# Attention in a fused attention and experts kernel: smaller array pieces for scores and values, v in longer packets, TensorE's work of an iteration in two long runs

## The chip, the cores and the metric

The kernel runs on one core of one Trainium2 chip. The metric is the device time in microseconds of one execution. TensorE (PE) does matmuls and transposes and writes PSUM; VectorE (DVE) and ScalarE (ACT) read PSUM and do the elementwise work; GpSimd (POOL) copies and clears in SBUF; SyncE (SP) issues most DMAs.

## The reference

Attention inside chunks of 64 positions, then a top-1 mixture of experts over the tokens.

```python
# q, k, v: [8 batches, 8 heads, 576 positions, 64]; chunks of 64 positions
scores = scale * np.matmul(q_c, k_c.transpose(0, 1, 2, 4, 3))
scores = scores - np.max(scores, axis=-1, keepdims=True)
attn = np.exp(scores)
attn = attn / (np.sum(attn, axis=-1, keepdims=True) + 1e-09)
out = np.matmul(attn, v_c)                       # -> x: [8, 576, 512]
# experts: 8 of them, w1 512x1024, w2 1024x512
logits = x @ w_gate
local_gate = 1.0 / (1.0 + np.exp(-(x @ w_local)))
# per token: its own best expert, or the previous token's where local_gate >= 0.5
h = np.maximum(x[b, s] @ w1[e], 0.0)
out[b, s] = p[e] * (h @ w2[e])
```

## The kernel before

The 4608 tokens are 18 blocks of 256 (`NS`), each of four 64-position chunks. Attention runs as a software pipeline over blocks. In iteration i of the loop (lines 780 to 796, i from 1 to 15) stand: scores of block i+1 (`s`), transposes of the probabilities of block i (`tp`), values of block i-1 (`va`), transposes of q and k of block i+2 (`tq`, `tk`), transposes of the output x of block i-2 (`tx`), the router's logits of block i-3 (`ra`), and the regrouping copy of q and k of block i+3 (`pr`). A string of such names (`PAR["steady"]`) is the order in which the pieces are written down, and each of PE, DVE, ACT and POOL executes its own part in that order. SP's order is made by the scheduler. At the end of an iteration q and k of block i+4 and v of block i+1 are loaded, in some iterations a quarter of an expert's weights, and in iterations 4 to 11 one half of a w1 piece is split into a high part (ACT, line 101) and a low part (DVE, line 102). The names `h0` to `h3` are places at which the steps of the routing of the first half are put in, from iteration 11 on.

Scores (line 202): for a pair of heads the transposed q of a chunk is the stationary operand, 128 rows (two heads of 64) by 64 columns. The transposed k is laid out in `kbd` as a block diagonal: head 0 in rows 0 to 63 and columns 0 to 63, head 1 in rows 64 to 127 and columns 64 to 127, the rest zeros. One matmul of 128 columns gives both heads. Two chunks go to output partitions 0 to 63 and 64 to 127. Values (line 248) are built alike: probabilities of two chunks as the contraction's 128 rows, and `v` with zero blocks and two columns of ones for each half (`DV` = 66, 132 columns a head pair of chunks); the column of ones gives the sum by which `norm` divides. The zeros and ones are written once by POOL at the start (lines 491 to 500); the loads of v fill the rest in packets of 256 bytes.

Each quarter of transposes (four of 128 x 128) fills one of three PSUM buffers (`ps_tr`), and a copy takes it out (line 161). `o`, the output of the values, is one PSUM tile for four heads, used twice a block: the second half may start when `norm` has read the first. `sc`, the scores, is one tile.

Before the loop a longer order string (`PAR["start"]`) plays the first blocks; after it `PAR["drain"]` mixes the last blocks with the first expert's work; then come the expert tiles, 507 us, to the end.

Of the kernel before, what the change touches and what calls it, by code (L numbers as in the profile page):

```python
# [8 lines left out]
F32 = mybir.dt.float32  # L9
# [15 lines left out]
P = 128  # L25
# [4 lines left out]
DV = D + 2  # L30
TA = 18
# [23 lines left out]
    "p0": "AVAAAVVV",  # L55
    "p1": "AAVA",
    "p2": "PAAA",
    "p3": "PPVP",
    "t0": "VVAVAA",
    "t1": "AAAAVA",  # L60
    "t2": "AAVAVA",
    "steady": (
        "s*4 tp*3 va h0 tp*3 va tp*2 va*2 ra h1 tk*8 s*4 tq s tq*7 va ra va tx*2 va*2 h2 pr*3 h3 tx s "
        "tx*5 pr "
    ),
# [5 lines left out]
def tile_attention_then_moe(ctx: ExitStack, tc, q, k, v, wg, wl, w1, w2, out):  # L71
# [13 lines left out]
    wg9 = cpool.tile([P, 4, 32], F32, name="wg9")  # L85

# [51 lines left out]
    def load_v(i):  # L138
        vt = vbuf[i % NV]
        for ch in range(4):  # L140
            t0 = 256 * i + 64 * ch
            b, s0 = t0 // S, t0 % S
            nc.sync.dma_start(
                vt[64 * (ch // 2):64 * (ch // 2) + 64, ch % 2, :, ch // 2, 0:D],
                v[b, :, s0:s0 + 64, :].rearrange("h s d -> s h d"),
            )
        return vt

    def pair_heads(qk, engs, parts=1):
        hd, fns = [], []  # L150
        w = 4 // parts
        dsts = [pe2.tile([P, 4, 2, 2, D], F32, name=nm + "r", tag=nm + "r", bufs=1) for nm in "qk"]
        for g in range(0, 4, w):
            for n in range(2):
                sv = qk[n].rearrange("p (hp j) (r d) -> p hp j r d", j=2, r=2)
                for r in range(2):
                    fns.append(lambda n=n, g=g, sv=sv, r=r: evac(
                        engs[len(engs) // parts * (g // w) + 2 * n + r] if parts > 1 else engs[2 * n + r],
                        dsts[n][:, g:g + w, r], sv[:, g:g + w, :, r]))
        return dsts, fns  # L160
# [24 lines left out]
    def qk_transposes(hd, qT, kbd, engs=None):  # L185
# [3 lines left out]
        kv = kbd.rearrange("a h c j (p r) -> a h c j p r", r=2)  # L189
        for r in range(2):  # L190
            atoms += trans4(
                lambda n, r=r: hd[0][:, n, r].rearrange("p j d -> p (j d)"),
                [(engs[r], qv[:, :, :, r], lambda ps: ps)], fine)
        for r in range(2):
            atoms += trans4(
                lambda n, r=r: hd[1][:, n, r].rearrange("p j d -> p (j d)"),
                [(engs[2 + 2 * r + j], kv[64 * j:64 * j + 64, :, :, j, :, r],
                  lambda ps, j=j: ps[64 * j:64 * j + 64].rearrange("a h (c p) -> a h c p", c=4))
                 for j in range(2)], fine)
        return atoms  # L200

    def scores(qT, kbd, pr, fine=False):
        sc = ps_s.tile([P, 4, 2, 2, D], F32, name="sc")

        def group(hp, cc):
            for cp in range(2):
                ch = 2 * cc + cp
                nc.tensor.matmul(  # L208
# [21 lines left out]
        def shift():  # L230
            top(0, 16)
            down(0, 16)
# [773 lines left out]
```

## Time and profile before

| what | value |
|---|---|
| median of 3 runs | 738.26 us (737.48 to 740.91) |
| profiled execution | 740.17 us, span 738.4 us |
| start, to the loop's first scores | 28.66 us |
| attention loop, 15 iterations | 152.25 us |
| drain | 50.09 us |
| experts | 507.40 us |
| one iteration in the middle (118.34 to 128.58 us) | 10.24 us |

The table's lower rows are stretches between instructions in the timeline, in the profiled execution. In the profile PE stands for matmuls and transposes, PEld for loading stationary operands (it overlaps PE). A row of the timeline merges neighbouring instructions of one kind on one engine: start, time from the first's start to the last's end, what it writes and reads, how many. `128*64` is the size of the array piece, rows by columns, and the next numbers are the moving operand. The end of a matmul includes the way through the array, so a stretch of work is read from one row's start to the next row's start.

### The profile page before, as it was taken

How to read it: one execution, taken by the hardware profiler on the slowest of the kernel's cores; microseconds unless marked ns; L12 is line 12 of the kernel's file. 1: busy time of each engine (PE TensorE's matmuls, PEld its weight loads, DVE VectorE, ACT ScalarE, POOL GpSimd, SP SyncE). 2: the span in 40 equal slices, each digit the busy share in tenths (PEclk: the TensorE clock that was granted, in tenths of full speed). 3: DMA queues.
4: the chain of work that ended last, by engine and by line, in shares of the span. 5: the costliest groups of instructions: out<-in, count | busy, mean ns of one | idle time of the engine just before them, and what ended most of it. 6: DMA issues, size and time to landing. Idle time of an engine off the chain costs nothing. (4 is left out here: it accounts for less than half of the span.)

```text
span 738.4 us, 14770 instructions
## 1 busy us (share of the span) xinstructions
PE 697.4 (94%) x4442; PEld 537.0 (73%) x4442; DVE 386.3 (52%) x853; ACT 302.6 (41%) x486; POOL 164.0 (22%) x191
## 2 busy tenths in 40 slices
PE   4899999999999999999999999999999999999982
PEld 3677666667677788686888887778887888777861
DVE  4555667777678465455323364563487332455320
ACT  3777777766532144153222441532463222432210
POOL 6110111023004122232212132322234111232100
PEclk9999999999999999999999999999999999999986
DMA  8989999997653114544111154441176310234100
GB/s 197 202 173 239 232 230 228 238 238 168 192 176 112 48 46 133 171 143 142 60 32 52 39 154 159 144 140 60 46 243 205 108 60 31 67 123 158 34 33 15
DMA packets 102918, 97.34 MB, mean 132 GB/s; under 512 B 42672, under 2 KB 79536, under 8 KB 102768
## 3 DMA queue, kind: packets, MB, share of 16 engines
q1 hardware_dynamic: 96608, 75.70, 41.0%
q0 software_dynamic: 6160, 19.85, 7.9%
q8 instruction: 69, 1.13, 0.7%
q14 instruction: 81, 0.66, 0.3%
HBM read 76.48 MB, written 19.56 MB: 130 GB/s over the span
## 5 line engine op out<-in xcount | busy, mean ns | idle before, releaser
L663 PE MATMUL y<-w2h,hp 128*128 128x512 f32 x608 | 204.7, 407 | 10.0 <-DVE hp L613 6.1
L649 PE MATMUL h<-w1h,xp 128*128 128x512 f32 x608 | 178.3, 403 | 0.0
L663 PEld LDWEIGHTS y<-w2h,hp 128*128 128x128 f32 x608 | 115.7, 191 | 39.1 <-DVE hp L613 8.3
L649 PEld LDWEIGHTS h<-w1h,xp 128*128 128x128 f32 x608 | 111.4, 189 | 23.9 <-ACTq L887 0.2
L663 PE MATMUL y<-w2l,hp 128*128 128x512 f32 x304 | 121.8, 401 | 0.0
L722 POOL DMA_INDIRECT out<-ysb,sidx x38 | 41.2, 1085 | 275.2 <-DVEq L887 187.9
L649 PE MATMUL h<-w1l,xp 128*128 128x512 f32 x304 | 95.8, 396 | 0.0
L612 ACT CAST hp<-tr 128x512 fp32r<-128x512 f32 x76 | 41.2, 589 | 107.3 <-PE tr L610 101.1
L613 DVE TENSOR_TENSOR xp<-tr,xp 128x512 fp32r<-128x512 f32 x39 | 27.0, 692 | 104.6 <-ACTq L887 67.1
L721 DVE TENSOR_SCALAR ysb<-y,ppr 128x512 f32<-128x512 f32 x35 | 26.2, 748 | 94.1 <-PE y L663 81.0
L649 PEld LDWEIGHTS h<-w1l,xp 128*128 128x128 f32 x304 | 57.1, 188 | 14.6 <-DVEq L887 0.4
L663 PEld LDWEIGHTS y<-w2l,hp 128*128 128x128 f32 x304 | 58.2, 191 | 12.4
L702 ACT ACTIVATE hsb<-h 128x1024 f32<-128x1024 f32 x35 | 35.9, 1027 | 66.9 <-PE h L649 64.3
L635 ACT ACTIVATE pex<-pex 128x8 f32<-128x8 f32 x38 | 8.0, 210 | 120.8 <-DVE pex L634 120.8
L613 DVE TENSOR_TENSOR hp<-tr,hp 128x512 fp32r<-128x512 f32 x76 | 49.3, 686 | 13.5 <-ACT hp L612 10.1
L257 PE MATMUL o<-v,pT 128*64 128x132 f32 x576 | 54.0, 293 | 1.8 <-DVE xs L272 1.8
L102 DVE TENSOR_TENSOR w1l<-raw,w1h 128x1024 fp32r<-128x1024 f32 (+1 forms) x29 | 41.0, 1433 | 19.7 <-ACT w1h L101 19.7
L166 POOL COPY qr<-qt 128x512 f32<-128x512 f32 x31 | 18.2, 616 | 127.8 <-PE tr L174 84.9
L616 POOL DMA_INDIRECT xg<-x_d,gidx x36 | 36.7, 1020 | 41.1 <-issue 23.4
L208 PE MATMUL sc<-kbd,qT 128*64 128x128 f32 x576 | 40.9, 287 | 5.1 <-ACT kbd L164 4.4
L257 PEld LDWEIGHTS o<-v,pT 128*64 128x64 f32 x576 | 30.0, 135 | 18.5 <-issue 17.2
L164 ACT COPY kbd<-tr 64x512 f32<-64x512 f32 x53 | 31.5, 622 | 22.0 <-PE tr L174 15.9
(177 smaller groups left out, 903.4 us busy)
## 6 DMA issues: line engine op xcount, KB each, us to landing
raw<-in_moe_w SPq DMA_DIRECT2D x72, 512.0 KB, 3.8
x_d<-xs SPq DMA_DIRECT2D x18, 521.0 KB, 4.1
v<-in_v SPq DMA_DIRECT2D x72, 128.0 KB, 5.8
qt<-in_q SPq DMA_DIRECT2D x11, 512.0 KB
kt<-in_k SPq DMA_DIRECT2D x11, 512.0 KB, 7.9
qt<-in_q SPq DMA_DIRECT2D x6, 256.0 KB, 6.6
kt<-in_k SPq DMA_DIRECT2D x6, 256.0 KB, 7.4
qt<-in_q SPq DMA_DIRECT2D x4, 384.0 KB
```

The lines of the kernel that those rows point to most:

```text
L102: (lo_eng or nc.vector).tensor_tensor(lo, raw, hi.bitcast(F32), ALU.subtract)
L164: eng.copy(dst, src)
L208: nc.tensor.matmul(sc[64 * cp:64 * cp + 64, hp, :, cc, :], qT[:, hp, 64 * ch:64 * ch + 64], kbd[:, hp, ch], start=True, stop=True,)
L257: nc.tensor.matmul(o[64 * cp:64 * cp + 64, hh, 0:2 * DV], pT[:, h, 64 * cp:64 * cp + 64], vt[:, cp, h].rearrange("p c d -> p (c d)"), star ...
L612: return [tr, lambda: nc.scalar.copy(hi, box["ps"]), lambda: V.tensor_tensor(lo, box["ps"], hi.bitcast(F32), ALU.subtract)]
L613: lambda: V.tensor_tensor(lo, box["ps"], hi.bitcast(F32), ALU.subtract)]
L616: nc.gpsimd.indirect_dma_start(out=dst, out_offset=None, in_=src, in_offset=bass.IndirectOffsetOnAxis(ap=gidx[t].bitcast(U32), axis=0))
L649: nc.tensor.matmul(hs[:, j], xs[a][:, c], W1[w][c][:, 512 * j:512 * j + 512], start=(c == 0 and n == 0), stop=(c == 3 and n == 2))
L663: nc.tensor.matmul(y, hx[f // 4][a][:, f % 4], W2[w][c][:, f % 2, :], start=(f == 0 and n == 0), stop=(f == 7 and n == 2))
L702: nc.scalar.activation(hsb, hs.rearrange("p j f -> p (j f)"), AF.Relu)
L721: either(mix, lambda: V.tensor_scalar(ysb, y, pr, None, ALU.mult), lambda: y_mixed(ysb, y, ym, pr))
L722: nc.gpsimd.indirect_dma_start(out=out, out_offset=bass.IndirectOffsetOnAxis(ap=sidx[t].bitcast(U32), axis=0), in_=ysb, in_offset=None, bo ...
```

## The change

Scores. k is transposed into a plain `kT`, and each head is a matmul of its own on a piece of 64 rows and 64 columns: 32 matmuls of 64 moving columns instead of 16 of 128. The two heads of a pair write different PSUM banks (`sc` has the head index j first). The pairing of heads changes from (2n, 2n+1) to (n, n+4).

Values. A position pair is split into r = 0 and 1, so that a piece has 32 rows. v has no zero blocks; two positions lie side by side with a column of ones before and after, `1 + 64 + 64 + 1` columns, and each matmul takes 65 of them: the sum of r = 0 falls into the first column, that of r = 1 into the last. Four small matmuls with `tiny` open each half and put 1e-9 there. 64 matmuls of 65 columns and 8 small ones stand for 16 of 132. `norm` adds the two sums (a reduce of two) in place of adding the 1e-9. v is loaded as eight DMAs of 64 KB in packets of 512 bytes in place of four of 128 KB in packets of 256.

Probabilities. `pr` has two buffers instead of one; subtracting the maximum is four instructions of 256 columns, because the result is written in the order that the 32-row pieces need.

Order. In the loop the values' first half comes first, then scores, router, the values' second half, and then all transposes as one run. ACT takes all PSUM copies, POOL all regrouping copies. At the start the big clears are gone, q and k of block 0 are regrouped in four copies instead of eight, and v of blocks 0 and 1 is loaded right behind q and k of the same block.

```diff
-    "steady": (
-        "s*4 tp*3 va h0 tp*3 va tp*2 va*2 ra h1 tk*8 s*4 tq s tq*7 va ra va tx*2 va*2 h2 pr*3 h3 tx s "
-        "tx*5 pr "
-    ),
+    "steady": "va*4 h0 s*8 ra h1 va*4 s h2 tp*8 tq*8 tq*8 tx*8 s ra h3 pr*4 ",
...
-    vbuf = [pa1.tile([P, 2, H, 2, DV], F32, name=f"v{i}") for i in range(NV)]
-    kbuf = [pe1.tile([P, 4, 4, 2, D], F32, name=f"kbd{i}") for i in range(2)]
+    vbuf = [pa1.tile([P, 2, 4, DV], F32, name=f"v{i}") for i in range(NV)]
...
-            nc.sync.dma_start(
-                vt[64 * (ch // 2):64 * (ch // 2) + 64, ch % 2, :, ch // 2, 0:D],
-                v[b, :, s0:s0 + 64, :].rearrange("h s d -> s h d"),
-            )
+            for hh in range(2):
+                p0 = 64 * hh + 32 * (ch // 2)
+                nc.sync.dma_start(
+                    vt[p0:p0 + 32, ch % 2, :, 1:1 + 2 * D],
+                    v[b, 4 * hh:4 * hh + 4, s0:s0 + 64, :].rearrange("h (p r) d -> p h (r d)", r=2),
+                )
...
-                nc.tensor.matmul(
-                    sc[64 * cp:64 * cp + 64, hp, :, cc, :],
-                    qT[:, hp, 64 * ch:64 * ch + 64],
-                    kbd[:, hp, ch],
-                    start=True, stop=True,
-                )
+                for j in range(2):
+                    nc.tensor.matmul(
+                        sc[64 * cp:64 * cp + 64, j, h, cc, :],
+                        qT[64 * j:64 * j + 64, h, 64 * ch:64 * ch + 64],
+                        kT[64 * j:64 * j + 64, h, :, 32 * ch:32 * ch + 32],
+                        start=True, stop=True,
+                    )
...
+        def down(j):
+            for c in range(2):
+                nc.vector.tensor_tensor(
+                    pr[:, :, :, j, c], sc[:, j, :, c].rearrange("p h (r k) -> p h r k", r=2),
...
+            for r in range(2):
+                for cp in range(2):
+                    for cc in range(2):
+                        rows = slice(64 * j + 32 * cc, 64 * j + 32 * cc + 32)
+                        nc.tensor.matmul(
+                            o[64 * cp:64 * cp + 64, cc, W * h + r:W * h + r + D + 1],
+                            pT[rows, h, r, 64 * cp:64 * cp + 64],
+                            vt[rows, cp, h, (D + 1) * r:(D + 1) * r + D + 1],
+                            start=False, stop=(h == 3 and r == 1),
+                        )
...
-        if i == 0:
-            nc.gpsimd.memset(kbuf[0], 0.0)
+        if i < 2:
+            vts[i] = load_v(i)
...
-    nc.gpsimd.memset(kbuf[1], 0.0)
-    for t in vbuf:
-        nc.gpsimd.memset(t, 0.0)
```

PE in the middle of the loop, one iteration of before, from its scores on (`tr<-ident,qr` and `kr` are transposes of q and k, `pr` of the probabilities, `xs` of x, `lg` the router):

```order
L208 MATMUL sc<-kbd_122,qT 64x2x64 x8
L174 MATMUL tr<-ident,pr 128x128 x3
L257 MATMUL o<-v_120,pT 64x132 x2
L174 MATMUL tr<-ident,pr 128x128 x3
L257 MATMUL o<-v_120,pT 64x132 x2
L174 MATMUL tr<-ident,pr 128x128 x2
L257 MATMUL o<-v_120,pT 64x132 x4
L300 MATMUL lg<-xT,wg_69 32x256 x4
L174 MATMUL tr<-ident,kr 128x128 x8
L208 MATMUL sc<-kbd_122,qT 64x2x64 x8
```

and one iteration of the change at the same place:

```order
L259 MATMUL o<-tiny 64x4 x4
L267 MATMUL o<-v_126,pT 64x65 x32
L203 MATMUL sc<-kT,qT 64x64 x32
L309 MATMUL lg<-xT,wg_69 32x256 x4
L259 MATMUL o<-tiny 64x4 x4
L267 MATMUL o<-v_126,pT 64x65 x32
L173 MATMUL tr<-ident,pr 128x128 x8
L173 MATMUL tr<-ident,qr 128x128 x8
L173 MATMUL tr<-ident,kr 128x128 x8
L173 MATMUL tr<-ident,xs 128x128 x8
L318 MATMUL lg<-ident,lT 128x128 x2
```

Kinds of work that alternated in short groups now stand in one group each; between the two halves of the values lie only scores and router.

DVE between two iterations, where a weight split falls in; of before (`rs` and `xs<-o,rs` are `norm`, `L<-lg` the router's end, `mx` and `pr<-sc` the shift by the maximum):

```order
L315 TENSOR_REDUCE L<-lg 128x18
L317 COPY xs<-L 128x2x9
L270 TENSOR_SCALAR rs<-o 128x8
L271 RECIPROCAL rs<-rs 128x8
L272 TENSOR_TENSOR xs<-o,rs 128x4x2x64
L102 TENSOR_TENSOR w1l_74<-raw_0_86,w1h_70 128x512
L270 TENSOR_SCALAR rs<-o 128x8
```

and of the change:

```order
L219 TENSOR_TENSOR pr<-sc,mx_1149 128x8x32 x2
L214 TENSOR_REDUCE mx_1153<-sc 128x8
L219 TENSOR_TENSOR pr<-sc,mx_1153 128x8x32 x2
L324 TENSOR_REDUCE L<-lg 128x18
L326 COPY xs<-L 128x2x9
L103 TENSOR_TENSOR w1l_81<-raw_0_93,w1h_77 128x512
L279 TENSOR_REDUCE rs<-o 128x8
L280 RECIPROCAL rs<-rs 128x8
L281 TENSOR_TENSOR xs<-o,rs 128x2x256
L314 COPY lT<-lg 128x256
```

The shift of an iteration now stands right ahead of the split, with no `norm` between them, and the next iteration's first `norm` behind both.

SP in one of the later iterations of the change (`x_d<-xs` writes x and the logits out, `raw` is a quarter of the next weights):

```order
L132 DMA qt<-in_q 128x8x128
L327 DMA x_d<-xs 128x2x521
L132 DMA kt<-in_k 128x8x128
L146 DMA v_127<-in_v 32x4x128 x8
L99 DMA raw_1_98<-in_moe_w 128x2x512
```

where before had x out first, and v in four:

```order
L318 DMA x_d<-xs 128x2x521
L131 DMA qt<-in_q 128x8x128
L131 DMA kt<-in_k 128x8x128
L143 DMA v_120<-in_v 64x8x64 x4
L98 DMA raw_0_90<-in_moe_w 128x2x512
```

q, and in some iterations k, moves ahead of the writing of x; v stays behind it and takes twice the issues.

More of the change, by code (lines that the diff above doesn't have):

```diff
@@ L29 @@
 HT = P // 2
-DV = D + 2
+W = D + 2
+DV = 2 * D + 2
 TA = 18
@@ L85, in tile_attention_then_moe @@
     wg9 = cpool.tile([P, 4, 32], F32, name="wg9")
+    tiny = cpool.tile([P, 68], F32, name="tiny")
+    nc.gpsimd.memset(tiny[:, 0:64], 0.0)
+    for p in range(0, P, 32):
+        nc.gpsimd.memset(tiny[p:p + 1, 0:64], 1.0)
+    nc.gpsimd.memset(tiny[:, 64:68], 1e-9)
     w1h = [wpool.tile([P, F], F32R, name=f"w1h{c}") for c in range(4)]
@@ L249, in values @@
         box = {}
-        def group(g, hh):
-            h = 4 * g + hh
-            if hh == 0:
-                box["o"] = ps_o.tile([P, 4, 256], F32, name="o")
-            o = box["o"]
-            for cp in range(2):
-                nc.tensor.matmul(
-                    o[64 * cp:64 * cp + 64, hh, 0:2 * DV],
-                    pT[:, h, 64 * cp:64 * cp + 64],
-                    vt[:, cp, h].rearrange("p c d -> p (c d)"),
-                    start=True, stop=True,
-                )
-            if hh == 3 and not fine:
-                norm(g)
@@ L266, in norm, with group @@
-        def norm(g):
-                o = box["o"]
-                ov = o[:, :, 0:2 * DV].rearrange("p h (c d) -> p h c d", d=DV)
-                rs = pa2.tile([P, 4, 2], F32, name="rs")
-                nc.vector.tensor_scalar_add(rs, ov[:, :, :, D], 1e-9)
+        def group(j, h):
+            if h == 0:
+                o = box["o"] = ps_o.tile([P, 2, 512], F32, name="o")
+                for cp in range(2):
+                    for cc in range(2):
+                        rows = slice(64 * j + 32 * cc, 64 * j + 32 * cc + 32)
+                        nc.tensor.matmul(
+                            o[64 * cp:64 * cp + 64, cc, 0:4 * W].rearrange("p (h d) -> p h d", d=W)[:, :, W - 1],
+                            tiny[rows, 0:64], tiny[rows, 64:68], start=True, stop=False)
+            o = box["o"]
+            for r in range(2):
+                for cp in range(2):
+                    for cc in range(2):
+                        rows = slice(64 * j + 32 * cc, 64 * j + 32 * cc + 32)
+                        nc.tensor.matmul(
+                            o[64 * cp:64 * cp + 64, cc, W * h + r:W * h + r + D + 1],
[3 more added lines that the diff above has]
+                        )
+            if h == 3 and not fine:
+                norm(j)
@@ L279, in values @@
         out = []
-        for g in range(2):
-            out += [lambda g=g, hh=hh: group(g, hh) for hh in range(4)]
+        for j in range(2):
+            out += [lambda j=j, h=h: group(j, h) for h in range(4)]
             if fine:
-                out.append(lambda g=g: norm(g))
+                out.append(lambda j=j: norm(j))
         return out
@@ L495, in tile_attention_then_moe @@
             nc.sync.dma_start(wg9[:, :, 8:9], wl.rearrange("(c p) e -> p c e", p=P))
-    nc.gpsimd.memset(kbuf[1], 0.0)
-    for t in vbuf:
-        nc.gpsimd.memset(t, 0.0)
-        for cc in range(2):
-            nc.gpsimd.memset(t[64 * cc:64 * cc + 64, :, :, cc, D:DV], 1.0)
     with tc.manual_schedule(engines=MAN):
```

136 lines of the change are left out of this document (64 added, 72 removed), and 4 rows, old and new, of the table PAR.

## The prediction

> **What bounds the kernel now.** I read the page first, then the sums by stage, then TensorE's timeline in the stage that the change touches.
>
> ```profile
> span 738.4 us, 14770 instructions
> PE 697.4 (94%) x4442; PEld 537.0 (73%) x4442; DVE 386.3 (52%) x853; ACT 302.6 (41%) x486; POOL 164.0 (22%) x191
> ```
>
> ```profile
> core 0: us, PE busy (x) PEld busy (x) DVE busy (x) ACT busy (x) POOL busy (x), PEclk, DMA share, GB/s
> 0.00:28.66 28.66, 15.16 (x121) 12.55 (x121) 15.38 (x21) 15.70 (x29) 13.96 (x45) 1.00 1.03 202
> 28.66:180.91 152.25, 151.45 (x1589) 105.79 (x1589) 101.26 (x227) 109.25 (x185) 23.40 (x40) 1.00 1.02 217
> 180.91:231.00 50.09, 47.89 (x395) 35.89 (x395) 35.88 (x125) 18.62 (x31) 7.96 (x10) 1.00 0.53 151
> 231.00:738.40 507.40, 482.87 (x2341) 382.77 (x2340) 233.83 (x484) 159.05 (x243) 118.67 (x97) 0.98 0.31 100
> ```
>
> The rows are the start, the attention loop (15 iterations), the drain and the experts. In the loop PE is busy 151.45 of 152.25 us, so what PE is given there is the time, as long as nobody keeps it waiting. DVE and ACT have about 30% free. The last stage, 507 us, is not edited; I leave it as it is. The profiled execution took 740.17 us, of which 738.4 are the span; the median of the runs is 738.26. All differences below are made against this execution and taken off the median.
>
> One iteration of the loop, PE alone (start, length, records; each score or value matmul leaves two records, a transpose one):
>
> ```profile
> 118.34 1.09 PE L208 MATMUL sc<-kbd,qT 128*64 128x128 f32 x16
> 119.37 0.55 PE L174 MATMUL tr<-ident,pr 128*128 128x128 f32 x3
> 119.85 0.45 PE L257 MATMUL o<-v,pT 128*64 128x132 f32 x4
> 120.22 0.55 PE L174 MATMUL tr<-ident,pr 128*128 128x128 f32 x3
> ...
> 121.44 0.67 PE L257 MATMUL o<-v,pT 128*64 128x132 f32 x8
> 122.05 0.64 PE L300 MATMUL lg<-xT,wg 128*32 128x256 f32 x8
> 122.62 1.09 PE L174 MATMUL tr<-ident,kr 128*128 128x128 f32 x8
> 123.64 1.09 PE L208 MATMUL sc<-kbd,qT 128*64 128x128 f32 x16
> ...
> 126.81 0.44 PE L174 MATMUL tr<-ident,xs 128*128 128x128 f32 x2
> 127.17 0.67 PE L257 MATMUL o<-v,pT 128*64 128x132 f32 x8
> 127.78 0.87 PE L174 MATMUL tr<-ident,xs 128*128 128x128 f32 x6
> 128.58 0.33 PE L208 MATMUL sc<-kbd,qT 128*64 128x128 f32 x2
> ```
>
> Read from start to start. Eight transposes take 1.02 us (122.62 to 123.64), two take 0.36 (126.81 to 127.17): 0.11 each, and **0.14 to 0.15 us per run**, whatever its length. Values say the same: 8 records 0.61, 4 records 0.37, so 0.06 a record and 0.13 a run. The L300 row shows pieces side by side: 8 records of 256 columns in 0.57 us; without the run's 0.14 that is two waves of four, 0.215 each, or 0.84 ns a column, however many pieces a wave has. Scores (two pieces of 128 columns, 0.11 a wave) and values (two of 132, 0.12) fit it. The iteration has 17 runs: 17 x 0.15 + 34 transposes x 0.11 + 16 score waves x 0.11 + 16 value waves x 0.12 + 2 x 0.215 = 10.4 us; the trace has 10.24.
>
> **The change, part by part.**
>
> PE in the loop. The 17 runs become 5 (values, scores, router, values, transposes): 12 x 0.15 = 1.8 us saved. Transposes and router stay. Scores are 32 matmuls, 64 records of 64 columns, four pieces at a time if the row pieces run side by side as the column pieces do: 16 waves of 64 x 0.84 = 0.054, which I take as 0.06: 0.96 us instead of 1.76. Values are 64 matmuls of 65 columns and 8 small ones that seed the sums, 144 records, 36 waves of 0.06: 2.16 us instead of 1.92. Sum: 0.75 + 3.74 + 0.96 + 2.16 + 0.43 = **8.04 us**, 2.2 below 10.24 (two per cent of it model error). The trace has no row piece. From below a wave is 0.054; from above look at the densest run there is:
>
> ```profile
> 179.66 0.61 PE L581 MATMUL tr<-qv,rh 128*128 128x12 bf16 x18
> 180.13 0.85 PE L174 MATMUL tr<-ident,xs 128*128 128x128 f32 x6
> ```
>
> 18 matmuls of 12 columns in 0.47 us, 26 ns each, on one piece. Four at 26 ns make a wave of 0.104. And if row pieces took turns, four would be two waves, 0.12. I take 0.06, since in the router's row four records do share one 0.215 wave; both other ends are rivals. [...]
>
> What keeps PE waiting then. Now all of an iteration's evacuations follow one run, and DVE stands between the two value halves, which share the tile o. Durations:
>
> ```profile
> 122.16 0.17 DVE L270 TENSOR_SCALAR rs<-o 128x8 f32<-128x8 f32 x1 [1.31 <-PE o L257]
> 122.36 0.20 DVE L271 RECIPROCAL rs<-rs 128x8 f32<-128x8 f32 x1
> 122.60 0.69 DVE L272 TENSOR_TENSOR xs<-o,rs 128x512 f32<-128x512 f32 x1
> 123.21 0.41 DVE L305 COPY lT<-lg 128x256 f32<-128x256 f32 x1
> 118.03 1.06 ACT L164 COPY xT<-tr 128x512 f32<-128x512 f32 x2
> ```
>
> ```profile
> L219 DVE TENSOR_REDUCE mx<-sc 128x8 f32<-128x512 f32 x4 | 2.6, 687 | 7.5 <-PE sc L208 7.5
> L222 DVE TENSOR_TENSOR pr<-sc,mx 128x512 f32<-128x512 f32 x4 | 2.7, 677 | 0.0
> L102 DVE TENSOR_TENSOR w1l<-raw,w1h 128x512 fp32r<-128x512 f32 x8 | 5.5, 691 | 13.2 <-ACT w1h L101 13.2
> L228 ACT ACTIVATE pr<-pr 128x1024 f32<-128x1024 f32 x15 | 15.8, 1057 | 3.1 <-DVE pr L222 3.1
> L101 ACT CAST w1h<-raw 128x512 fp32r<-128x512 f32 x8 | 5.0, 629 | 0.0
> L166 POOL COPY qr<-qt 128x512 f32<-128x512 f32 x31 | 18.2, 616 | 127.8 <-PE tr L174 84.9 <-DMA qt<-in_q 19.1 <-PE lg L309 10.0
> ```
>
> Let T be the start of the transposes. A normalisation is 1.13 us (122.16 to 123.29), so the second half's ends at T+1.3. The shift is now two maxima (0.65 in a row) and four subtractions of 256 columns (0.42, as the 256-column copy; not in the trace; from below 0.34, half of a 512 row, from above its whole 0.68): 3.0 us, to T+4.3. ACT alone copies eight quarters out at about 0.5 (two in 1.06 with the tail), from T+0.8 to T+4.8; PE makes a quarter in 0.44 and has three buffers, so it loses some 0.25. Then the exponential, to T+5.85. PE leaves the transposes at T+4.1, the first value half at T+5.35, and with scores (1.1) and router (0.6) asks for the second half at T+7.05. DVE has o's first half normalised at T+6.6: no wait, with 0.45 to spare. But in iterations 4 to 11 a weight split is queued on DVE ahead of that normalisation: it waits for ACT's cast, which stands behind the exponential: T+6.45, split to T+7.15, normalisation to T+8.3, and **PE waits 1.25 us** in each of the eight following iterations. [...]
>
> Loop: 6.8 and 7.8 us for the first two iterations (no x transposes or router yet), 2 x 8.3, 8 x 9.45, 3 x 8.3: 131.7. From iteration 11 on routing steps stand between, and one of their transposes now follows a normalisation: I allow 2.5, and 2 for waits that I can't place (allowances, read from no row). Sum 136 against 152.25: **16 us off**.
>
> The loads.
>
> ```profile
> 2.00:9.00 7.00, 0.05 (x1) 0.08 (x2) 5.19 (x3) 1.54 (x5) 6.84 (x9) 1.00 1.01 274
> 12.20 3.27 SPq L143 DMA_DIRECT2D v<-in_v  x4
> ```
>
> Between 2 and 9 us only 512 byte packets move, at 274 GB/s: 30 ns a packet and engine. An iteration brings 2.1 MB (q, k, v, and x_d out), 2.6 with weights: 7.7 and 9.6 us at that rate, against 8.3 and 9.45. Close, but weights come in 8 iterations only, and q and k are fetched two iterations ahead. The loop of before moves 217 GB/s x 152.25 us = 33 MB; in 136 us that is 243 GB/s. v is eight issues instead of four: an issue took some 0.5 us with little before it (0.8 in the row), so SP needs 4 to 6 us for them, behind x_d. v is due one iteration after: I count nothing, and keep the price as a rival.
>
> The start.
>
> ```profile
> 4.93 3.66 POOL L498 MEMSET v<- 128x2112 f32 x2
> 3.81 5.21 DVE L166 COPY qr<-qt 128x256 f32<-128x256 f32 x2 [3.81 <-DMA qt<-in_q]
> 8.95 0.87 PE L174 MATMUL tr<-ident,qr 128*128 128x128 f32 x3 [8.95 <-POOL v L500]
> 28.66 1.09 PE L208 MATMUL sc<-kbd,qT 128*64 128x128 f32 x16 [1.53 <-ACT kbd L164]
> ```
>
> PE's first transpose waits until 8.95 us, with DVE's copies stretched over 5.21 us while POOL clears the buffers. The clears go; q and k of chunk 0 are 1.05 MB, 3.8 us at 274 GB/s from 2 us on, so they are there at about 6 and the transposes begin near 7. What is late next is data: v of chunks 0 and 1 (1.05 MB, 3.8 us) now stands before q and k of chunk 2, which land near 20, and POOL copies them in 4 x 0.62. The loop begins at about 23.5, not 28.66: **5 us off**. Drain: value groups 4 waves of 0.06 instead of 2 of 0.12, plus seeds, and PE has 2.2 us idle there already: 1 us on. Sum: 16 + 5 - 1 = 20.
>
> **The rivals.**
>
> *Issue floor*: 26 ns a record, waves of 0.104. 52 waves x 0.044 more make an iteration of 10.35; the split wait is covered by the longer scores. The loop is 8.5 + 9.5 + 13 x 10.35 + 2 for the routing = 154.6, 2.3 on; start 5 off, drain 2 on: 738. For it: L581. Against: the router's row.
>
> *Row pieces take turns* (the slower end): waves of 0.12, 52 x 0.06 more, an iteration of 11.4; loop 9.5 + 10.5 + 13 x 11.4 + 2 = 170, 18 on; start 5 off, drain 2 on: 753. It decides from a wave of about 0.1 up. No row of before has a row piece, so nothing speaks for or against but the column pieces.
>
> *v comes late*: if the mix of loads gets 225 GB/s, nearer to the loop's 217 than to the 274 of the start, 33 MB take 147 us, 11 more than forecast: 729. For it: a DMA share of 1.02 already. Against: that share has v in 256 byte packets.
>
> *No split wait* (the exponential free earlier): 8 x 1.25 us less, and waves of 0.054 another 2: 706.
>
> **How the numbers follow.** Forecast 738.3 - 20 = **718**, by itself 711 to 724: 0.55. v late 0.15, issue floor 0.11, taking turns 0.12, faster still 0.07. The range reaches from 706 to 740, leaving out the turns and a little below. A measurement tells about 0.5%, 3.7 us, from no change: faster 0.78 (forecast, late v, the faster case), same 0.09, slower 0.13 (turns, and the tail of the floor).
>
> **What would show it.** Five PE runs to an iteration; L203 records 64 in 1.1 us and L267 records in runs of 64 in 1.0 to 1.1 (0.104: 1.7; turns: 2). DVE's normalisation before the second value half ending the longest PE waits in iterations 5 to 12, of about 1.2 us, and none in 3 and 4. The loop's first row near 23.5 and the experts unchanged at 507 us. I am wrong if a wave takes over 0.1, if PE's waits before L267 end on DMA, or if the drain grows by more than 3 us.

## The result, and the profile after

The changed kernel takes **789.5 us** (median of 4 runs, 786.7 to 792.0), the kernel before 739.2 beside it: a ratio of 1.068, 95% interval 1.063 to 1.073. The prediction said 718.

From the page of the changed kernel (span and busy times, the rows by 40 slices for TensorE's granted clock, and the DMA queue of the kind `instruction`: packets, MB, share):

```profile
span 789.9 us, 20116 instructions
PE 707.6 (90%) x7034; PEld 577.7 (73%) x7034; DVE 372.7 (47%) x896; ACT 271.9 (34%) x432; POOL 179.1 (23%) x230
...
PEclk9786877778887999999999999999999999999996
...
q8 instruction: 90, 1.47, 0.8%
```

and by stage. The loop reaches from its first value run to that of the sixteenth block, 27 to 236 us, and is shown in two rows; before is below it, with its loop in one row:

```profile
0.00:27.00 27.00, 14.71 (x196) 12.72 (x196) 7.54 (x17) 8.10 (x13) 10.96 (x54) 0.95 0.87 204
27.00:180.00 153.00, 121.30 (x2861) 110.38 (x2860) 67.46 (x178) 65.70 (x111) 26.92 (x47) 0.76 0.66 169
180.00:236.00 56.00, 41.61 (x973) 35.04 (x973) 30.35 (x102) 21.68 (x37) 17.16 (x27) 0.85 0.60 162
236.00:789.90 553.90, 529.95 (x3017) 419.60 (x3009) 267.37 (x602) 176.38 (x272) 124.03 (x103) 0.98 0.31 103
```

```profile
30.20:183.50 153.30, 152.50 (x1607) 106.84 (x1606) 102.47 (x232) 109.45 (x186) 24.42 (x41) 1.00 1.02 217
183.50:738.40 554.90, 528.17 (x2698) 416.41 (x2697) 268.32 (x601) 176.87 (x272) 125.61 (x106) 0.98 0.33 104
```

The whole loss is in the loop: 209 us instead of 153 for the fifteen iterations, while what follows takes 554 instead of 555 and the start is 3 us shorter. In the first 153 us of the loop TensorE is busy for 121 only, and is granted 0.76 of its clock. The last row of the page's excerpt will matter later: 90 packets of instructions on this queue, where before has 69.

One iteration of the changed kernel, 13.99 us from the first row to the last (timeline of all engines, some rows):

```profile
94.52 1.14 PE L267 MATMUL o<-v,pT 32*64 32x65 f32 x64
...
95.06 0.37 SPq L327 DMA_DIRECT2D x_d<-xs  x1
...
95.59 1.16 PE L203 MATMUL sc<-kT,qT 64*64 64x64 f32 x64
...
96.68 0.64 PE L309 MATMUL lg<-xT,wg 128*32 128x256 f32 x8
...
97.29 0.20 DVE L280 RECIPROCAL rs<-rs 128x8 f32<-128x8 f32 x1
99.66 0.69 DVE L281 TENSOR_TENSOR xs<-o,rs 128x512 f32<-128x512 f32 x1 [2.17 <-DMA x_d<-xs]
...
100.50 0.39 PE L259 MATMUL o<-tiny 32*64 32x4 f32 x8 [3.18 <-DVE xs L281]
...
100.70 2.02 PE L267 MATMUL o<-v,pT 32*64 32x65 f32 x64
...
102.66 1.97 PE L173 MATMUL tr<-ident,pr 128*128 128x128 f32 x8
...
104.42 1.91 PE L173 MATMUL tr<-ident,qr 128*128 128x128 f32 x8
...
108.51 0.91 PE L267 MATMUL o<-v,pT 32*64 32x65 f32 x48
```

The runs and pieces are as predicted: five runs, 64 score records in 1.09 us (95.59 to 96.68), 64 value records in 1.07 (94.52 to 95.59). Then TensorE stands for 3.2 us. The second value half needs the tile `o`; DVE has the reciprocals at 97.5 but can't multiply into `xs`, because that buffer, one of three, still waits to be written out to `x_d`. That write, the last step of the iteration before, was issued only at 95.06 and landed at about 99.6. After the wait the value half takes 1.96 us and eight transposes 1.76: TensorE runs at half its clock. The granted clock, in windows cut where it changes:

```profile
85.77:92.60 6.83, 6.32 (x92) 6.23 (x93) 4.46 (x11) 2.25 (x4) 0.37 (x1) 0.50 0.92 253
92.60:99.42 6.82, 4.72 (x160) 3.84 (x158) 1.49 (x5) 3.70 (x7) 1.97 (x4) 1.00 0.38 120
99.42:106.25 6.83, 5.75 (x89) 5.66 (x90) 4.32 (x10) 1.79 (x3) 0.00 (x0) 0.50 0.76 205
106.25:116.49 10.24, 6.49 (x237) 5.51 (x236) 2.95 (x10) 4.06 (x7) 2.35 (x4) 1.00 0.41 123
116.49:119.90 3.41, 3.41 (x18) 3.41 (x17) 3.27 (x8) 1.89 (x4) 0.00 (x0) 0.50 0.58 165
```

In each of the two full-speed stretches a wait for `x_d` begins, and each is followed by one at half speed. From 60 to 180 us the wait comes eight times:

```profile
PE o L259 <- DVE xs L281: 22.7, 8, 3.7
```

(us in total, times, the longest). This was theory T1: the wait for `x_d` idles TensorE, the idling lowers the clock, the lowered clock doubles the transposes. Its rivals were R1, that small pieces lower the clock by themselves, and R2, that other waits (split, v, evacuations) would do it as well.

### The profile page after: what moved, and what is told of

Same layout as the page of the kernel before. It is cut to its first block, busy times and chain, and to the rows that moved or that the text cites. A ratio compares the mean times of both kernels' runs of the same rounds, so it can differ in the third digit from the quotient of the medians.

```text
span 789.9 us, 20116 instructions
## 1 busy us (share of the span) xinstructions
PE 707.6 (90%) x7034; PEld 577.7 (73%) x7034; DVE 372.7 (47%) x896; ACT 271.9 (34%) x432; POOL 179.1 (23%) x230
## 5 line engine op out<-in xcount | busy, mean ns | idle before, releaser
L667 PE MATMUL y<-w2h,hp 128*128 128x512 f32 x608 | 202.6, 403 | 8.9 <-DVE hp L617 6.4
L267 PE MATMUL o<-v,pT 32*64 32x65 f32 x2304 | 54.5, 252 | 8.0 <-issue 6.9
L163 ACT COPY pT<-tr 128x512 f32<-128x512 f32 x36 | 20.9, 585 | 110.9 <-PE tr L173 110.8
L267 PEld LDWEIGHTS o<-v,pT 32*64 32x64 f32 x2304 | 49.0, 164 | 9.6 <-issue 8.0
L617 DVE TENSOR_TENSOR hp<-tr,hp 128x512 fp32r<-128x512 f32 x76 | 49.3, 685 | 13.8 <-ACT hp L616 11.2
L165 POOL COPY qr<-qt 128x512 f32<-128x512 f32 x34 | 20.0, 618 | 133.4 <-DMA qt<-in_q 53.6
L173 PE MATMUL tr<-ident,qr 128*128 128x128 f32 x144 | 32.0, 395 | 11.0 <-ACT qr L163 8.3
```

The costliest lines, as they stand in the source:

```text
L163: eng.copy(dst, src)
L173: nc.tensor.transpose(box["ps"][:, n], src_of(n), ident)
L267: nc.tensor.matmul(o[64 * cp:64 * cp + 64, cc, W * h + r:W * h + r + D + 1], pT[rows, h, r, 64 * cp:64 * cp + 64], vt[rows, cp, h, (D + 1) ...
L617: lambda: V.tensor_tensor(lo, box["ps"], hi.bitcast(F32), ALU.subtract)]
L667: nc.tensor.matmul(y, hx[f // 4][a][:, f % 4], W2[w][c][:, f % 2, :], start=(f == 0 and n == 0), stop=(f == 7 and n == 2))
```

## The experiments

An overview first. Each run is compared with runs of before taken beside it, whose medians were 737.3 to 739.2. "Iteration" is the mean of eight, from the fifth block's first value run to the thirteenth's in the timeline; the clock is that of the window from 60 to 140 us; "block stalls" are explained with the second group (among the gaps of over 0.6 us between the starts of TensorE's instructions from 30 to 225 us, the number of those at block starts, and their sum).

| run | us | ratio to before [95%] | iteration us | clock | block stalls |
|---|---|---|---|---|---|
| before | 739.2 | | 10.3 | 1.00 | 0 |
| after | 789.5 | 1.068 [1.063, 1.073] | 13.4 | 0.77 | 3, 8 us |
| xs4 | 778.9 | 1.053 [1.049, 1.056] | 13.1 | 0.80 | 16, 33 us |
| ra_early | 793.6 | 1.075 [1.069, 1.080] | 13.2 | 0.83 | 19, 41 us |
| fill | 803.3 | 1.088 [1.083, 1.092] | 13.4 | 1.00 | 6, 10 us |
| b_late | 742.7 | 1.004 [1.001, 1.007] | 11.2 | 0.98 | 0 |
| shift128 | 770.1 | 1.044 [1.042, 1.046] | 11.1 | 0.91 | 7, 19 us |
| noload | 761.1 | 1.034 [1.030, 1.039] | 10.1 | 0.98 | 7, 8 us |
| halves | 761.8 | 1.031 [1.027, 1.035] | 12.2 | 0.85 | 12, 23 us |
| halves_al | 758.8 | 1.029 [1.024, 1.033] | 10.9 | 0.96 | 12, 18 us |
| halves_al2 | 757.1 | 1.025 [1.021, 1.030] | 10.8 | 0.98 | 9, 14 us |
| halves_quiet | 756.5 | 1.024 [1.019, 1.029] | 9.9 | 1.00 | 2, 3 us |
| b_order | 753.3 | 1.020 [1.016, 1.024] | 12.3 | 0.94 | 0 |
| b_order2 | 737.3 | 1.000 [0.997, 1.003] | 10.2 | 1.00 | 0 |
| b_order_quiet | 744.8 | 1.010 [1.005, 1.016] | 9.6 | 1.00 | 0 |
| mixed | 743.6 | 1.008 [1.005, 1.011] | 11.1 | 0.94 | 3, 8 us |
| mixed2 | 740.0 | 1.003 [0.999, 1.006] | 11.1 | 0.96 | 3, 8 us |

noload, halves_quiet and b_order_quiet attend over other data, so other experts are chosen; from the 73rd matmul with `w1h` to the end of the span they take 498 to 500 us, the others 478 to 487 (before 484, the changed kernel 480, fill 487). Their loops can be compared, their totals can't.

### The wait for x_d, and the clock

**xs4**, a fourth buffer (and a tile moved to make room):

```diff
-        xss[i] = pa2.tile([P, 2, XR], F32, name="xs", bufs=3)
+        xss[i] = pa2.tile([P, 2, XR], F32, name="xs", bufs=4)
...
-    q8 = pc.tile([P, E, NT], F32, name="q8", bufs=1)
+    q8 = pa2.tile([P, E, NT], F32, name="q8", tag="xT", bufs=1)
```

> The changed kernel with four buffers for xs in place of three (and q8 in the place of xT, to make room). Theory T1 (the second value half waits for DVE, DVE for x_d's write of the block four earlier to land, PE then stands for 3 us and its clock drops to half): that wait is gone, the granted clock between 30 us and the end of the loop is above 0.95, an iteration in the middle takes 8.3 to 9.5 us instead of 14.0, 720 to 735 us. Rival R1 (many small pieces lower the clock by themselves): the clock in the loop stays at 0.8 or below and only the 3 us of the wait go, 11 us an iteration, 745 to 760 us. Rival R2 (weight split, v and evacuations keep PE waiting enough): clock between 0.8 and 0.95, 735 to 755 us, with other waits of over 1 us in every iteration.

**ra_early**, the router's end (and the write of `x_d`) ahead of the transposes:

```diff
-    "steady": "va*4 h0 s*8 ra h1 va*4 s h2 tp*8 tq*8 tq*8 tx*8 s ra h3 pr*4 ",
+    "steady": "va*4 h0 s*8 ra h1 va*4 ra s h2 tp*8 tq*8 tq*8 tx*8 s h3 pr*4 ",
```

> The changed kernel with the second part of the router (two transposes, the sums, the write of x_d) moved ahead of the transposes, three buffers as they were: the same remedy without a buffer. T1: the write is issued some 6 us earlier and has landed, or nearly, when DVE asks for its buffer; clock above 0.95, 720 to 738 us. R1: clock as in the changed kernel (0.8 or below in the loop), 745 to 760 us.

**fill**, work for TensorE in the place where it idles:

```diff
             if not fine:
+                for _ in range(32):
+                    nc.tensor.transpose(lg[:, 1, 0:P], ident, ident)
                 cp()
```

> The changed kernel, its wait left as it is, with 32 transposes of the unit matrix that nobody reads put behind the router's four matmuls in 13 iterations: 3.5 us of work for TensorE (32 x 0.11) at the place where it stands idle. T1: TensorE no longer idles, the clock stays above 0.95, and though work is added an iteration takes about 11.7 us instead of 14.0: 755 to 770 us. R1 or no link between idling and clock: the added work changes nothing or comes on top, 789 to 820 us.

**b_late**, the kernel before with its write of `x_d` at the end of the iteration:

```diff
-        "s*4 tp*3 va h0 tp*3 va tp*2 va*2 ra h1 tk*8 s*4 tq s tq*7 va ra va tx*2 va*2 h2 pr*3 h3 tx s "
-        "tx*5 pr "
+        "s*4 tp*3 va h0 tp*3 va tp*2 va*2 ra h1 tk*8 s*4 tq s tq*7 va va tx*2 va*2 h2 pr*3 tx s "
+        "tx*5 ra h3 pr "
```

> The kernel before, with the second part of the router (and so the write of x_d) moved to the end of the iteration as in the changed kernel, pieces as they were. T1: DVE waits for the landing in every iteration (4.4 us behind the issue, the first normalisation comes some 3 us after it), PE with it, by 1 to 2 us; if such a wait suffices the clock falls with the old, large pieces too: 755 to 790 us, clock in the loop below 0.95. R1: PE waits 1 to 2 us an iteration at full clock, 750 to 765 us and clock above 0.98 in the loop.

Measured: xs4 778.9, ra_early 793.6, fill 803.3, b_late 742.7. xs4 lies outside the forecasts of all three theories, and so does ra_early: the wait for `x_d` is gone in both, xs4 wins back only 11 of the 50 us, and ra_early none. The timeline of TensorE in xs4 shows what came instead:

```profile
103.75 1.14 PE L267 MATMUL o<-v,pT 32*64 32x65 f32 x64
104.82 0.34 PE L203 MATMUL sc<-kT,qT 64*64 64x64 f32 x8
107.27 1.23 PE L203 MATMUL sc<-kT,qT 64*64 64x64 f32 x56 [2.10 <-issue]
```

After the eighth of 64 score records, in the midst of a run, TensorE stands for 2.1 us, and the profile names nobody it waits for ("issue"). ra_early has such stalls too.

fill settles the clock, though not the time (its time lies where R1 had it, its clock where T1 had it). With the same small pieces and 3.5 us of added work the clock is 1.00 from 60 to 140 us, where the changed kernel has 0.77: so it is idling that lowers it, not the pieces (R1 falls). But no time is won. DVE still waits for the landing; from 60 to 140 us the waits hold

```profile
DVE xs L281 <- DMA x_d<-xs: 21.1, 6, 4.4
```

but the added work now covers this wait:

```profile
60.00:140.00 80.00, 74.77 (x1752) 65.67 (x1752) 37.88 (x98) 32.88 (x60) 13.85 (x24) 1.00 0.90 216
...
108.47 3.71 PE L312 MATMUL lg<-ident 128*128 128x128 f32 x32
112.43 0.29 PE L259 MATMUL o<-tiny 32*64 32x4 f32 x8 [0.25 <-DVE xs L281]
```

TensorE is busy for 74.8 of the 80 us and waits for DVE's `xs` once, for those 0.25 us. Its own work is now some 12 us an iteration (the 11.9 us from 112.54 to 124.45 have no wait in them), and in the loop there are six block stalls, 10 us in all. So fill shows what the idling does to the clock, and not what a full clock is worth. Its loop takes 208 us, as that of the changed kernel does.

b_late missed both its forecasts: the later write costs 0.4%, and the clock stays at 0.98. DVE waits for the landing there too, 3.5 us in five waits from 60 to 140 us, but TensorE waits for none of them: transposes of q and k and scores stand between its two value halves. The late write does its harm in the new order around it.

### The stalls without a releaser

A stall in the middle of a run suggests the instructions themselves. Number all instructions of TensorE in the trace, loads of weights and waits for semaphores included, and set beside them the 16 KB packets of the instruction queue (21 packets more than before for 5346 instructions more on the span's lines, all engines together: 255 to a packet). The gaps of over 0.6 us in xs4, from the start of one instruction to the start of the next, then fall into two kinds. These are four of the first:

```
instruction  rest by 256  gap us  ends at  last 16 KB packet ended
       1729          193    3.26    61.08     59.57
       3265          193    1.03    99.08     97.65
       3521          193    2.32   107.27    105.99
       4289          193    1.59   123.92    122.62
```

In xs4 16 of 22 gaps stand at a number that leaves 193, and every one ends 1.2 to 1.8 us behind the end of such a packet; in ra_early it is 19 of 22. Theory T2: TensorE's program comes in blocks of 256 instructions, and TensorE runs out of it. The changed kernel has some 250 matmul records an iteration, each with a load of weights, 506 instructions in all, nearly two blocks; before has about 220, less than one. The dense part, 128 instructions in 1.07 us, eats a block in 2.1 us, and a packet alone takes about one (0.88 to 1.52 us in the changed kernel, median 1.00). Rival R3: a wait on data that the profile doesn't name. Four runs on this.

**shift128** moves the grid of blocks and nothing else (once, ahead of the loop, on xs4):

```diff
+    pad = trp()
+    for _ in range(32):
+        nc.tensor.matmul(pad[0:64, 0:4], tiny[0:32, 0:64], tiny[0:32, 64:68], start=True, stop=True)
     for i in range(1, NS - 2):
```

> The kernel of four xs buffers with 32 matmuls of 4 columns that nobody reads (128 instructions of TensorE) put once ahead of the loop; the loop's own instructions and waits are the same, word for word. Theory T2 (TensorE's program comes in blocks of 256 instructions by a 16 KB transfer; a stall without releaser stands at a block's first instruction until about 1.4 us behind the end of such a packet): the stalls leave the tenth score matmul and stand 32 instructions into the first value half and at the start of the second, still 193 behind a multiple of 256; the stretch of transposes then lies behind the trigger of its fetch and hides it, so one of two stalls an iteration goes: 760 to 775 us. Rival R3 (a data wait that the profile doesn't name, tied to the place in the program): stalls stay behind about 10 score matmuls, 779 to 783 us.

**noload** leaves the loads of q, k and v out of the loop (on xs4):

```diff
-            qk[i + 4] = load_qk(i + 4)
+            qk[i + 4] = kept[3 + (i + 1) % 2]
...
-            vts[i + 1] = load_v(i + 1)
+            vts[i + 1] = vbuf[(i + 1) % NV]
```

> The kernel of four xs buffers without the loads of q, k and v inside the loop (its blocks read the tiles loaded at the start, so that the attention of later blocks is that of other data); weights and x_d move as before. T2 with the fetch delayed by the data packets: packets of 16 KB start sooner and take less than 0.95 us, stalls at block starts shrink from 1 to 3.4 us to 0.5 to 1.5, 745 to 765 us. T2 with the fetch asked for late in its block whatever the load: stalls at most a third shorter, 765 to 778 us. R3 with a wait on data: no stalls at all, 720 to 735 us.

**halves** spreads the transposes over both blocks (on xs4):

```diff
-    "steady": "va*4 h0 s*8 ra h1 va*4 s h2 tp*8 tq*8 tq*8 tx*8 s ra h3 pr*4 ",
+    "steady": "va*4 h0 s*4 ra h1 tp*8 tx*8 va*4 ra s*4 s h2 tq*8 tq*8 s h3 pr*4 ",
```

> The kernel of four xs buffers in another order of the iteration: values half, scores half, router, probability and x transposes; values half, router's end, scores half, q and k transposes (seven runs in place of five, two stretches of transposes in place of one, each half of the iteration 256 instructions). No padding: the blocks begin some 16 instructions into the score halves. T2: each block now holds slow transposes, so that its 256 instructions last 4 us wherever it begins; stalls of under 1.5 us, iteration of 9.5 to 11.5 us, 740 to 765 us. Rival R2 (evacuations and the shift keep TensorE waiting, the order as dense as can be is best): more waits on ACT, 780 us or more.

**halves_al** is halves with the padding of shift128 (36 matmuls) and one such matmul in each router step.

> The same order with the blocks lined up: 36 matmuls of 4 columns ahead of the loop (144 instructions) and one per iteration against the drift, so that a block begins with a values half and ends in transposes. T2 with a trigger a third to a half into the block: the fetch passes behind the transposes, hardly any stall, iteration of 8.5 to 9.5 us at full clock, 725 to 740 us. R3: as the run without padding, within 4 us.

Measured: 770.1, 761.1, 761.8 and 758.8. In shift128, 128 instructions that do nothing make the kernel 9 us faster (a ratio of 1.044 instead of 1.053), although the loop's first value run comes at 36.2 us instead of 26.4: iterations of 11.1 us instead of 13.1. Seven stalls are left at the rest 193, now in other places of the program: the two after 68 us stand in the router's matmuls, at 88.6 and 98.5, not in the value halves as expected, and from 100 to 160 us there is none. The scores pass in one piece there:

```profile
115.58 1.14 PE L267 MATMUL o<-v,pT 32*64 32x65 f32 x64
116.65 1.16 PE L203 MATMUL sc<-kT,qT 64*64 64x64 f32 x64
117.75 0.64 PE L309 MATMUL lg<-xT,wg 128*32 128x256 f32 x8
119.44 0.39 PE L259 MATMUL o<-tiny 32*64 32x4 f32 x6 [1.05 <-DVE xs L281]
```

R3 falls: a wait on data would not move with the count of instructions. In noload the block stalls shrink from 33 us to 8, the clock is back at 0.98 and an iteration takes 9.92 us in the quiet stretch, so most of the stall comes with the loads: the packet of a dense block starts 1.4 to 3.8 us behind the block's first instruction in xs4 (to 165 us), and 1.1 to 1.8 us in noload. It takes about one, as it did with the loads (less than 0.95 was expected), and TensorE goes on 1.2 to 1.5 us behind it: 3.7 to 4.2 us from block to block in noload, where 256 dense instructions are 2.1 us of work. From 60 to 145 us every block of noload begins so close behind a packet, also where the gap is under 0.6 us, so the packets may pace this loop too. What asks for a packet, and when, the trace does not show. The total of noload, 761, lies within the first of its three forecasts, but it stands on other routing. halves lies in T2's range of 740 to 765 us, by luck: its iteration is 12.2 us, not 9.5 to 11.5, and its twelve stalls are 1.9 us on average, where under 1.5 was expected. halves_al missed T2's range: 3 us below halves is what R3 had, though its iterations fell from 12.2 to 10.9 us, since here too the padding delayed the first value run by 7 us, and 12 stalls are left in both.

### Fewer runs, and fewer instructions

The prediction's largest term was the saving by fewer runs. **b_order** gives the kernel before that order alone:

```diff
-        "s*4 tp*3 va h0 tp*3 va tp*2 va*2 ra h1 tk*8 s*4 tq s tq*7 va ra va tx*2 va*2 h2 pr*3 h3 tx s "
-        "tx*5 pr "
+        "va*4 h0 s*8 ra h1 va*4 ra h2 tp*8 s tq*8 tk*8 tx*8 s h3 pr*4 "
```

> The kernel before, pieces, buffers and start as they were, with its iteration in five or six runs: values, scores, router, values, router's end, probability, q, k and x transposes (the maxima and the shift behind the probability transposes, since there is one pr). About 212 TensorE instructions an iteration, under one block of 256. T2 with the prediction's step on runs right (0.15 us each): no stall at a block start, clock above 0.97, 8.5 to 9.3 us an iteration in place of 10.24, 718 to 730 us. If fewer runs bring nothing because evacuations then come in one heap: waits on ACT and DVE of over 1 us an iteration, 736 to 750 us.

**mixed** has the new scores and start with the old values: 276 instructions an iteration. In short:

```diff
-                    kT[64 * j:64 * j + 64, h, :, 32 * ch:32 * ch + 32],
+                    kT[64 * j:64 * j + 64, h, 64 * ch:64 * ch + 64],
...
-    vbuf = [pa1.tile([P, 2, 4, DV], F32, name=f"v{i}") for i in range(NV)]
+    vbuf = [pa1.tile([P, 2, H, 2, DV], F32, name=f"v{i}") for i in range(NV)]
...
-    "steady": "va*4 h0 s*8 ra h1 va*4 s h2 tp*8 tq*8 tq*8 tx*8 s ra h3 pr*4 ",
+    "steady": "va*4 h0 s*8 ra h1 va*4 ra h2 tp*8 s tq*8 tq*8 tx*8 s h3 pr*4 ",
```

> The changed kernel's scores (64 x 64 pieces, k without zero blocks) with the values, the loads and the zero blocks of v of before (132 columns, 128 rows), start order of the changed kernel, order of the iteration as in b_order: 138 matmul records an iteration in place of 250, 276 instructions in place of 506. T2: the block of 256 lasts 7 us or more, its dense part (scores, 128 instructions in 1.1 us) is short, hardly any stall at block starts, 8.0 to 9.0 us an iteration, 708 to 724 us. Rival (the 64 x 64 pieces themselves bring the stalls or the clock down, whatever the count of instructions): stalls of over 1 us in the scores in most iterations, 745 us or more. Rival (loads bound it, v in 256 byte packets at the 217 to 238 GB/s of before): no stalls at block starts, TensorE waits for DMA, 9.5 to 10.2 us an iteration, 726 to 738 us.

Measured: 753.3 and 743.6, both outside all their forecasts. mixed has three block stalls, of 1.1 to 3.8 us, and the wait that b_order has, up to 1.4 us. b_order has no block stall, and is slower than before all the same. Its waits from 60 to 140 us, then DVE and TensorE in one iteration:

```profile
DVE w1l L101 <- ACT w1h L100: 25.8, 6, 4.4
PEld o L256 <- issue: 16.0, 9, 3.0
PE o L256 <- DVE xs L271: 12.8, 6, 2.6
```

```profile
102.75 0.69 DVE L101 TENSOR_TENSOR w1l<-raw,w1h 128x512 fp32r<-128x512 f32 x1 [4.38 <-ACT w1h L100]
103.36 0.16 DVE L269 TENSOR_SCALAR rs<-o 128x8 f32<-128x8 f32 x1
...
104.62 1.12 PE L256 MATMUL o<-v,pT 128*64 128x132 f32 x16 [1.95 <-DVE xs L271]
105.68 0.44 PE L308 MATMUL lg<-ident,lT 128*128 128x128 f32 x2
105.95 1.76 PE L173 MATMUL tr<-ident,pr 128*128 128x128 f32 x8
107.51 1.91 PE L173 MATMUL tr<-ident,qr 128*128 128x128 f32 x8
```

This is the wait that the prediction saw: DVE's weight split stands for ACT's cast behind the exponential, the normalisation behind the split, TensorE behind both, in the iterations with a split. It is 1.9 to 2.6 us here, and behind some of these waits the clock falls with the old, large pieces as well: eight transposes take 1.6 us at 105.95, and the window has 0.94 of the clock.

```profile
95.86:106.10 10.24, 7.82 (x99) 6.35 (x98) 4.21 (x10) 6.71 (x12) 1.18 (x2) 1.00 1.02 200
106.10:109.51 3.41, 3.41 (x19) 3.41 (x17) 3.24 (x6) 1.85 (x4) 0.00 (x0) 0.50 0.40 131
109.51:129.99 20.48, 15.04 (x193) 12.45 (x192) 9.20 (x20) 13.31 (x23) 2.36 (x4) 1.00 1.06 203
```

The wait before 104.62 has half clock behind it, the next one, before 117.31 and of the same length, has none: of the seven waits of 1.9 us or more four have.

**b_order2** and **mixed2** move that one step, in an order that is otherwise the same:

```diff
-        "va*4 h0 s*8 ra h1 va*4 ra h2 tp*8 s tq*8 tk*8 tx*8 s h3 pr*4 "
+        "va*4 h0 s*8 ra h1 va*4 sp ra h2 tp*8 s tq*8 tk*8 tx*8 s h3 pr*4 "
...
+        opt["sp"] = (lambda: [split_w1]) if 4 <= i < 12 else None
```

> The run b_order with one step moved: the split of the weights (ACT's cast, DVE's subtraction), which stood behind the exponential at the end of the iteration and so ahead of the next normalisation on DVE, now stands behind the second value half. If the loss of b_order is DVE waiting for ACT's cast and TensorE for the normalisation behind it (1.9 us in eight iterations, and the lower clock after it): those waits go, clock above 0.98, 9.2 to 9.8 us an iteration, 728 to 738 us. If the order itself loses (evacuations in one heap): within 5 us of the 753 of b_order.

> The run mixed with the same step moved. If what is left over the 8 us of work an iteration in mixed is that wait (1.4 us, eight times) and two or three stalls at block starts: 8.0 to 9.0 us an iteration, clock above 0.97, 720 to 732 us, faster than both kernels. If loads bound it (256 byte packets): TensorE waits for v and q, 9.3 to 10 us an iteration, 736 to 744 us.

Measured: 737.3 and 740.0. In b_order2 the waits and the low clock are gone from 60 to 140 us, 16 us are won back, and the result is the time of before: 1.000 [0.997, 1.003]. It is what was expected of the move, though the iteration is 10.2 us and not 9.2 to 9.8. mixed2 has no split wait, but small ones on v and `x_d` and three block stalls, the longest 4.6 us; its time lies where the loads as the bound had it, its iteration of 11.1 us above both forecasts. Neither beats before.

### What the loads cost

**halves_quiet** and **b_order_quiet** leave q, k and v out of the loop as noload does, with the split moved and, in halves, the padding at the program's start. **halves_al2** is halves_quiet with its loads.

> The run halves_al with the padding moved to the program's start, the weight split behind the second value half, and without the loads of q, k and v in the loop (later blocks then attend over the first tiles' data). If loads and program blocks are all that stood between the prediction's sum and the chip: 8.3 to 9.0 us an iteration (8.04 of work, two runs and a matmul more), clock 1.0, stalls at block starts under 0.5 us, 718 to 730 us. If the pieces or runs cost more than their terms: 9.3 us or more an iteration with TensorE busy throughout, 735 us or more.

> The same with its loads. If the padding ahead of the loop cost the 7 us by which the first value half came late, and the split the waits of its eight iterations: 740 to 750 us, stalls at block starts as in halves_al. If loads alone set the pace: 750 to 760 us.

> The run b_order2 without the loads of q, k and v in the loop: old pieces in six runs. If the loads (v in 256 byte packets) took what the fewer runs save: 8.4 to 9.0 us an iteration instead of 9.2 to 10.6, 718 to 728 us. If a run is cheaper than the 0.15 us of the prediction, or evacuations hold it up: 9.2 us or more, 730 to 738 us.

Measured: 756.5, 757.1 and 744.8, all above the first of their forecasts (the first and the third with the longer last stage). halves_al2 has its first value run back at 27.3 us, and wins 2 us where 8 or more were expected; it lies where "loads alone set the pace" had it. halves_quiet lies in its second range, and its iteration too, but TensorE is not busy throughout. The iterations tell more. halves_quiet repeats 9.63 to 9.67 us; TensorE in it:

```profile
101.57 1.09 PE L176 MATMUL tr<-ident,pr 128*128 128x128 f32 x8
...
103.63 1.14 PE L270 MATMUL o<-v,pT 32*64 32x65 f32 x64
...
107.91 1.14 PE L270 MATMUL o<-v,pT 32*64 32x65 f32 x64
109.84 0.69 PE L206 MATMUL sc<-kT,qT 64*64 64x64 f32 x32 [0.79 <-DVE rs L282]
...
111.24 1.09 PE L176 MATMUL tr<-ident,pr 128*128 128x128 f32 x8
```

0.85 us of it is a wait (the score tile is still being read by the shift when the next scores come), 8.8 is work: the prediction's 8.04 with two runs more (0.30) and one small matmul (0.2) would be 8.54. b_order_quiet repeats 9.48 with 0.5 of waiting, 9.0 of work, where before takes 10.24. So the iterations miss their expectations (8.3 to 9.0, 8.4 to 9.0) by a wait each, and halves_quiet by 3% of work besides; the pieces and runs cost about what the prediction said. With the loads the same orders take 10.8 and 10.2 us an iteration, unevenly.

## Why the prediction was wrong

**Runs and pieces: right.** Five runs; scores take 1.09 us, where 0.96 and the run's 0.15 were forecast, both value halves with their small matmuls 2.4, where 2.16 and twice 0.15 were; the row pieces run side by side (17 ns a record, where two column pieces alone would make 27 at the prediction's 0.84 ns a column), so the rivals "issue floor" and "row pieces take turns" fall by the rows at 94.52 and 95.59. The new pieces' work, added up from noload's rows without its waits, is 2.4 us for the values, 1.1 scores, 0.6 router, 3.8 and 0.3 transposes: 8.2 against 8.04. The old pieces' work went from 10.24 to 9.0 us with the new order (b_order_quiet, without the loads), 11 runs fewer at 0.11 us instead of 0.15. One slip in the prediction's sum is of no weight: 8.3 and a wait of 1.25 are 9.55, not 9.45.

**"DVE has o's first half normalised at T+6.6: no wait": this is the step that failed.** It took DVE's own queue and nothing else. The multiplication also needs a free buffer of `xs`, and the new order sets the write that frees it to the end of the iteration: DVE asks for the buffer 2.4 us behind the write's issue, and the landing takes 4.5. The listing of SP's queue in the part on the change shows the write moved; what waits for its landing was not asked. That made 2.8 us an iteration on average, 2.3 to 3.7, and not 0. The sign that the prediction named shows it as well: the wait ends on DVE, but it stands in iteration 4 already (2.3 us, before 71.80 us), where none was to be.

**The clock was taken as 1.0 throughout.** That held in before, whose TensorE is busy for 152.5 of the loop's 153.3 us at a clock of 1.00. Most waits for `x_d` brought a stretch at half clock behind them (not all: one of 2.5 us, before 182 us, did not); fill, the same pieces without the idling, has 1.00 from 60 to 140 us. What the half clock costs by itself wasn't measured apart.

**Instructions were counted as time on the array only.** 250 records an iteration are 506 instructions, and from one dense block of 256 to the next it took 3.7 to 4.2 us even without the loads (noload), where the work is 2.1. With the wait for `x_d` removed, the iteration is still 13.1 us (xs4), with 33 us of block stalls in the loop and a clock of 0.80, and moving the blocks' grid changes it to 11.1 (shift128). No term of the sum and no rival held it.

**The split wait: the mechanism right, and hidden.** 1.25 us in eight iterations were forecast; the changed kernel waits longer for `x_d` at the same place, so it does not show there. It shows in mixed (1.4 us at most) and b_order (up to 2.6), and goes when the split is moved.

**"v is due one iteration after: I count nothing": wrong in kind.** TensorE seldom waits for v, but without the loads an iteration falls from 13.1 to 9.9 us (noload against xs4): the packets of the program then start earlier (1.1 to 1.8 us behind a block's first instruction in place of 1.4 to 3.8), and the writes of `x_d` land 3.0 to 3.3 us behind their issue, where the changed kernel has 4.1 and 4.5. The rival "v comes late" named the resource, not the way, and gave 729.

**Start and rest.** The loop's first row, now a value run, comes at 27.0, where 23.5 was forecast; before has its first scores at 28.66 and its first value run at 30.2. So 2 to 3 us are off instead of 5. The last stage is 4 us shorter without an edit there (480 against 484 from the 73rd matmul with `w1h`), which stays open.

So where the loop was to be 16 us shorter, it is 55 us longer, and no rival came near: the slowest said 753. The work did shrink, by 2 us an iteration; what TensorE waits for grew by more. How the 55 us divide between the wait, the half clock and the blocks was not measured apart, since taking the wait away brought more block stalls.

## What to carry to other kernels

When work is moved, follow every buffer that it frees, to the landing of the transfer that frees it, and ask who writes there next; a step that was harmless in the middle of an iteration can hold up the next one when it stands at the end (in the changed order TensorE waited 2.3 to 3.7 us for it, and b_late lost 0.4%). Cutting matmuls into small pieces multiplies instructions (here from about 220 to 506 an iteration): count them against blocks of 256, and look at dense stretches that fill a whole block while loads run (33 us of block stalls in xs4, 8 in noload without the loads). And TensorE busy for 99% of its loop held a clock of 1.00 here (before); behind a wait of 3.2 us in the changed kernel eight transposes took 1.76 us, where before takes 1.02.

## What the runs showed of the hardware

- The queue of the kind `instruction` moves packets of 16 KB, one more for every 255 instructions that the changed kernel has more than before. In 16 of 22 gaps of xs4 and 19 of 22 of ra_early TensorE stalled at a number that leaves 193 by 256, and such stalls, 99 in the twelve kernels for which the table counts any, ended 1.2 to 1.8 us behind the end of a packet. A dense block took 3.6 to 6.0 us to the next block's first instruction in ra_early, 3.7 to 4.2 in noload.
- The granted clock changed in steps of 3.41 us: the stretches in the rows above are one, two, three and six times that (3.41, 6.83, 10.24 and 20.48 us), at 0.5 or 1.0. In b_order four of seven waits of 1.9 to 2.6 us had half clock behind them; in the changed kernel one of 2.5 us had not. What decides between them isn't shown.
- Pieces of 64 x 64 and 32 x 64, four to a wave as the program lays them out: 64 records, with as many loads of weights, in 1.09 and 1.07 us (changed kernel, rows at 95.59 and 94.52), 17 ns each; 128-row pieces of 12 columns took 26 ns in before (L581).
